# A sixth pair of row tiles in block products, and the last slots of a fused attention and mixer kernel rearranged

## The chip, the cores and the metric

The kernel runs on one core of one Trainium2 chip. The metric is the device time of one execution in microseconds (us). The kernel takes and gives float32; inside, the operands of its matmuls are float16 and the sums float32. The engines are called TensorE (PE in the profile), VectorE (DVE), ScalarE (ACT), GpSimd (POOL) and SyncE (SP, which only issues transfers here).

## The reference

Cosine attention over 8 batches, 12 heads, 448 rows and 64 columns, then a mixer of two parts: one over the rows (tokens), one over the columns (channels).

```python
q_n = q / (norm(q) + 1e-6); k_n = k / (norm(k) + 1e-6)
attn = softmax(q_n @ k_n.T / tau)
x = (attn @ v), heads side by side                  # [8, 448, 768]
h = max(x.T @ w_tok1, 0) @ w_tok2                   # 448 -> 256 -> 448
u = x + h.T
out = u + max(u @ w_ch1, 0) @ w_ch2                 # 768 -> 1536 -> 768
```

## The kernel before

**Slots.** Two heads of a batch make a pair; there are 48 pairs, six to a batch. The loop runs over them, and pass i is called slot i here. The order of all instructions is written out by hand: each engine works through its own queue in the order of the program. In slot i TensorE makes the scores of pair i (`score`, `score_rest`; exponentials on ScalarE), attention times v of pair i-1 (`pv_rest`, `pv`; VectorE divides with `rec` and writes `x`), the token mixer's second layer of pair i-2 (`tok2`, VectorE writes `u`) and its first layer of pair i-1 (`tok1`, VectorE writes `rt`). `side` holds what the other engines do for later pairs: GpSimd casts v, squares k and scales k and q (`kq`), VectorE sums the squares, SyncE loads and transposes.

**The channel mixer fills the slots.** `WORK` says which parts go into which slot. `ch1(b, ct)` is one of the 12 column blocks of the first layer of batch b (six matmuls of 448 columns, ReLU on ScalarE into `gt`). `ch2(b, m, n)` is one half (384 columns) of the second layer for row tile m of batch b: 12 matmuls, `psF`, and a VectorE add of u. A row tile has 128 rows. Two batches have 896 rows, so tiles of an odd batch are shifted by 64, and tile (b, 3) holds the last 64 rows of batch b-1 and the first 64 of batch b. Its add of u was made in two parts of 64 partitions, from the u of either batch.

**Block products.** For a pair of row tiles r1 and r2, `sg_first` and `sg_second` replace the four halves by seven products of six matmuls of 384 columns each (`sg_prod`), from sums of the tiles (`sg_sum` on GpSimd, tiles sg0 to sg2) and sums of the weights (`tw`). `FIRST` and `SECOND` say in which slots. In the slot of `sg_first` stand product 1 (`psY`) and 2 (`psX`) ahead of score_rest, 6 behind it, and 7 behind tok1; in that of `sg_second` products 5 (`psZ`) and 4 (`psW`) ahead of score_rest and 3 (again `psZ`) near the end. VectorE adds each to the output rows (`osg`).

**PSUM.** Pool `ps` (tag "b") has two buffers of a bank, `ps2` (tag "s") three of two banks. A tile of a pool waits until the buffer's last reader is done: psO of the two heads, psX, psW, psU (tok2), psR (tok1) and psT (transposes of u) take turns in "b"; scores, psY, psZ and the tail's `px`, `py`, `pz` in "s".

**The tail.** Batches 6 and 7 have their first layer in block products too, over both batches at once, behind slot 47: `prod1`, in steps `p1` to `p7`, each for d = 0, 1, 2. They read sums of the weights (`fast_weights1`: n = 1 writes s1w, 2 writes s2w from it, 3 rewrites a quarter of wc1t, 4 writes s4w), and differences of u (`fast_x`: t1x to t4x). Pair 47's u is transposed on TensorE (`upose`) for them. `fast_g` makes the sums for the second layer (`s1g`, `s2g` first). One helper records most elementwise operations of VectorE and GpSimd, so that they share line 544 in the profile before; the tiles tell them apart.

Of the kernel before, what the change touches and what calls it, by code (L numbers as in the profile page):

```python
# [22 lines left out]
def kernel(  # L23
# [12 lines left out]
    nc = tc.nc  # L36
# [455 lines left out]
    def m_ch2(b, m, lo, hi, st, wide):  # L492
# [10 lines left out]
        def add(p0, p1, bb, slot):  # L503
            nc.vector.tensor_tensor(out=o[p0:p1, lo:hi].rearrange("p (j e) -> p j e", e=128),
                                    in0=psF[p0:p1, 0:hi - lo].rearrange("p (j e) -> p j e", e=128),
                                    in1=u16[bb][p0:p1, lo // 128:hi // 128, slot], op=ALU.add)

        if m < 3:
            add(0, 128, b, m + b % 2)
        else:  # L510
            add(0, 64, b - 1, 3)
            add(64, 128, b, 0)
# [101 lines left out]
    def u_shared():  # L614
        nc.sync.dma_start(out=u16[B1][0:64, :, 0], in_=u16[B0][0:64, :, 3])
# [89 lines left out]
    def sg_first(r1, r2):  # L705
# [22 lines left out]
        return head, middle, end  # L728
# [187 lines left out]
    with tc.manual_schedule():  # L916
# [154 lines left out]
        for i in range(NPAIR + 1, NP_ALL):  # L1071
# [48 lines left out]
            if second:  # L1120
                second[1]()
# [155 lines left out]
```

## Time and profile before

| | us |
|---|---|
| median of 3 runs | 378.15 |
| lowest, highest | 377.91, 379.19 |
| the profiled execution | 377.93 |
| its span, first to last instruction | 376.1 |
| TensorE busy | 360.6 |
| GpSimd busy | 293.4 |
| VectorE busy | 260.5 |
| ScalarE busy | 251.5 |

The profiled execution is one run; the durations of single instructions come from it. In a row of the timeline stand start, duration, engine, line, operation and tiles, and in brackets how long the engine had been idle and what ended that. A busy time of TensorE includes some 0.2 us in which a matmul's result is still under way; the chain counts from one result to the next. The mean granted clock of TensorE was 0.997 of full.

### The profile page before, as it was taken

What the parts mean: (1) busy time and instruction counts of PE and PEld (TensorE: products, weight loads), DVE (VectorE), ACT (ScalarE), POOL (GpSimd) and SP (SyncE); (2) the same over time, 40 slices, a digit from 0 to 9 for tenths busy, and PEclk for the clock granted to TensorE, in tenths of its full rate; (3) what the DMA queues carried; (4) which work ended last, traced back from release to release, by engine and by line L of the source; (5) the groups of instructions that cost most, each with busy time, mean ns of one, the idle gap of its engine ahead of it and who ended that gap; (6) DMA issues with size and microseconds to landing.
All of it is one profiled execution on the core that took longest, in us unless ns stands there. A gap on an engine that the chain in (4) does not pass through costs nothing.

```text
span 376.1 us, 10388 instructions
## 1 busy us (share of the span) xinstructions
PE 360.6 (96%) x4060; PEld 236.0 (63%) x4060; DVE 260.5 (69%) x589; ACT 251.5 (67%) x440; POOL 293.4 (78%) x405
## 2 busy tenths in 40 slices
PE   6788999999999999999999999999999969999995
PEld 5566666676666766666666766666666646556663
DVE  7789765776556763875864876646777698786873
ACT  5999887857788597666677755978688434265110
POOL 8899998989989987878766887469989962345753
PEclk9999999999999999999999999999999999999998
DMA  7999999988989798879898979979875713103344
GB/s 200 270 254 197 265 255 205 208 149 163 231 206 198 163 246 173 178 171 237 163 204 187 162 182 214 225 172 182 196 148 124 150 40 99 22 3 91 89 125 126
DMA packets 118224, 64.64 MB, mean 172 GB/s; under 512 B 74272, under 2 KB 114848, under 8 KB 118176
## 3 DMA queue, kind: packets, MB, share of 16 engines
q1 hardware_dynamic: 111984, 58.25, 71.1%
q0 software_dynamic: 5616, 5.21, 8.8%
q8 instruction: 31, 0.51, 0.6%
q10 hardware_dynamic: 576, 0.52, 0.5%
q14 instruction: 17, 0.14, 0.1%
HBM read 43.45 MB, written 11.01 MB: 145 GB/s over the span
## 4 chain that ended last, share of the span: by engine, by line
PE 86%; DVE 5%; ACT 5%; DMA 1%; issue 1%; POOL 0%; SPq 0%; DVEq 0%; ACTq 0%
PE psG L483 22%; PE psO L402 9%; PE psF L500 8%; PE psS L363 8%; PE psU L452 5%; PE psR L438 5%; PE psYo L790 4%; PE psY L686 3%; ACT pt L364 3%; PE psY L598 3%; PE psXo L790 3%; PE psZo L790 3%; PE psZ L686 2%; PE psZ L598 2%; PE psX L598 2%; PE psQ L370 2%
## 5 line engine op out<-in xcount | busy, mean ns | idle before, releaser
L364 ACT ACTIVATE pt<-psS 128x896 f16<-128x896 f32 (+1 forms) x156 | 135.7, 911 | 28.3 <-PE psS L363 28.2
L483 PE MATMUL psG<-ut,wc1t 128*128 128x448 f16 x432 | 90.1, 352 | 0.0
L316 POOL TENSOR_TENSOR kq<-kf,rn 128x384 f16<-128x384 f32 (+1 forms) x43 | 38.0, 885 | 35.0 <-DVE rn L293 34.2
L483 PEld LDWEIGHTS <-wc1t 128*128 128x128 f16 x432 | 40.4, 97 | 32.0
L486 ACT ACTIVATE gt<-psG 128x448 f16<-128x448 f32 x72 | 38.9, 541 | 30.6 <-PE psG L483 30.6
L280 DVE TENSOR_REDUCE ssq<-sq 128x15 f32<-128x960 f32 (+2 forms) x45 | 49.9, 1111 | 2.9 <-ACT sq L262 2.9
L441 DVE TENSOR_SCALAR rt<-psR 128x256 f16<-128x256 f32 x48 | 20.1, 418 | 43.6 <-PE psR L438 43.6
L363 PE MATMUL psS<-qk 64*128 64x448 f16 x312 | 41.2, 354 | 4.4 <-DVE qk L342 3.0
L316 POOL TENSOR_TENSOR kq<-qf,rn 112x512 f16<-112x512 f32 x41 | 42.8, 1044 | 2.8
L455 DVE TENSOR_TENSOR u<-psU,x 128x512 f16<-128x512 f32 x48 | 33.1, 689 | 12.4 <-PE psU L452 11.4
L402 PE MATMUL psO<-vt,pt 128*128 128x65 f16 (+1 forms) x1024 | 39.2, 194 | 0.0
L406 DVE TENSOR_TENSOR x<-psO,rec 128x256 f16<-128x256 f32 x82 | 34.8, 424 | 2.8
L402 PEld LDWEIGHTS <-pt 128*128 128x128 f16 (+1 forms) x1024 | 34.2, 97 | 3.5 <-issue 0.9
L500 PE MATMUL psF<-wc2t,gt 128*128 128x384 f16 x192 | 33.8, 326 | 0.0
L264 POOL TENSOR_TENSOR sq<-kf 128x384 f32<-128x384 f32 (+1 forms) x35 | 30.0, 857 | 0.1
L452 PE MATMUL psU<-rt,w2t 128*128 128x128 f16 x384 | 29.4, 220 | 0.6 <-POOL w2t L211 0.6
L452 PEld LDWEIGHTS <-w2t 128*128 128x128 f16 x384 | 24.8, 98 | 8.0 <-DVE rn L293 0.8
L438 PEld LDWEIGHTS <-w1t 128*128 128x128 f16 x384 | 24.8, 98 | 7.9 <-issue 2.1
L438 PE MATMUL psR<-x,w1t 128*128 128x128 f16 x384 | 29.3, 219 | 0.2 <-DVE u L455 0.2
L371 ACT ACTIVATE pt<-psQ 128x448 f16<-128x448 f32 x36 | 19.6, 544 | 12.3 <-PE psQ L370 12.2
L324 POOL TENSOR_SCALAR kq<-kr,rn 64x64 f16<-64x64 f32 x72 | 22.7, 315 | 3.6
L363 PEld LDWEIGHTS <-qk 64*128 64x128 f16 x312 | 12.6, 94 | 19.0 <-issue 6.3
(164 smaller groups left out, 654.5 us busy)
## 6 DMA issues: line engine op xcount, KB each, us to landing
qf<-in_q_dram SPq DMA_DIRECT2D x43, 224.0 KB, 3.9
vf<-in_v_dram SPq DMA_DIRECT2D x36, 192.0 KB, 3.6
kf<-in_k_dram SPq DMA_DIRECT2D x34, 192.0 KB, 3.7
wc1t<-in_moe_w_ch_dram POOLq DMA_DIRECT2D x4, 576.0 KB, 10.5
wc2t<-in_moe_w_ch_dram POOLq DMA_DIRECT2D x2, 1152.0 KB, 12.7
kf<-in_k_dram SPq DMA_DIRECT2D x9, 224.0 KB, 8.4
vf<-in_v_dram SPq DMA_DIRECT2D x9, 224.0 KB, 8.3
kr<-in_k_dram SPq DMA_DIRECT2D x24, 48.0 KB, 3.6
```

Source lines behind the costliest of these rows:

```text
L280: nc.vector.tensor_reduce(out=st["ssq"][0:n, sl], in_=st["sq"][0:n, sl], axis=AXX.X, op=ALU.add)
L316: eng.tensor_tensor(out=kq[0:p, a, 0:n].rearrange("p c g e -> p g c e"), in0=st["kq"[a]][:].rearrange("p (g c) e -> p g c e", g=2), in1=_b ...
L363: nc.tensor.matmul(psS[:, hh, 0:S], qk[hb, c * n:c * n + 128], qm[hb], start=True, stop=True)
L364: nc.scalar.activation(out=pts[i % 2][0:n, 2 * S * c:2 * S * (c + 1)].rearrange("p (h s) -> p h s", h=2), in_=psS[0:n, :, 0:S], func=AF.Ex ...
L402: nc.tensor.matmul(psO[:, m, 0:E + 1], pts[i % 2][0:n, at:at + 128], vt[0:n, i % HP, nch * hh + c, 0:E + 1], start=(old(i) and c == 0), st ...
L406: nc.vector.tensor_tensor(out=st["x"][:, :, hh * E:(hh + 1) * E], in0=psO[:, :, 0:E], in1=_bcast_free(rec[:], E), op=ALU.mult)
L438: nc.tensor.matmul(psR[:, tt], w1t[:, w1[m], tt * 128:(tt + 1) * 128], st["x"][:, m], start=(m == 0), stop=(m == 3))
L452: nc.tensor.matmul(psU[:, m], w2t[:, tt, lo:lo + 128], st["rt"][:, tt], start=(tt == 0), stop=(tt == TT - 1))
L483: nc.tensor.matmul(psG[:, 0:S], wc1t[:, dt, ct * 128:(ct + 1) * 128], ut[b][:, dt].rearrange("p m s -> p (m s)")[:, lo:lo + S], start=(dt ...
L486: nc.scalar.activation(out=gt[:, ct, (b % 2) * S:(b % 2 + 1) * S], in_=psG[:, 0:S], func=AF.Relu)
L500: nc.tensor.matmul(psF[:, 0:hi - lo], gt[:, ct, at:at + 128], wc2t[:, ct, lo:hi], start=(ct == 0), stop=(ct == CT - 1))
L790: nc.tensor.matmul(out[:, o:o + hi - lo], a[:, j], fast_w2(n, j)[:, lo:hi], start=(start and j == 0), stop=(j == HC - 1), skip_group_check ...
```

## The change

- Tiles (2, 0) and (3, 3) become a sixth pair `G[5]`: their four halves in slots 26, 32 and 33 go, and products 1, 2, 6, 7, 5, 4 stand in slot 33, product 3 in slot 34. Tile (3, 2) has both its halves in slot 32.
- The pairs in `AHEAD` (`G[4]` and `G[5]`) have products 5 and 4 at the end of the first slot and no longer in the second. Product 5 goes into a "b" bank and is added to both output tiles; product 3 starts a bank of its own (`psV`).
- The first layers of batches 2 to 4 are spread anew over slots 21 to 38, the pairs G[1] and G[2] move to slots 29, 30 and 37, 38, and their GpSimd sums with them. In slot 32 ScalarE squares k.
- `u_shared` now copies the 64 shared rows of u into the odd batch in slots 16, 28 and 40, so that the add of a shared tile is one instruction.
- In slot 47, s1g and s2g (`fast_g`) are made behind product 3, where they stood in slot 46, and `p1(0)` stands ahead of tok1(46). s1w (GpSimd) moves from slot 46 to 47, s2w (VectorE) from slot 47 to behind pv of pair 47, and s4w from GpSimd in slot 47 to VectorE behind the t's of the second block of u.

```diff
-        def add(p0, p1, bb, slot):
...
-        if m < 3:
-            add(0, 128, b, m + b % 2)
-        else:
-            add(0, 64, b - 1, 3)
-            add(64, 128, b, 0)
+        nc.vector.tensor_tensor(out=o[:, lo:hi].rearrange("p (j e) -> p j e", e=128),
+                                in0=psF[:, 0:hi - lo].rearrange("p (j e) -> p j e", e=128),
+                                in1=u16[b][:, lo // 128:hi // 128, (m + b % 2) % 4], op=ALU.add)
...
-    def u_shared():
-        nc.sync.dma_start(out=u16[B1][0:64, :, 0], in_=u16[B0][0:64, :, 3])
+    def u_shared(b=B1):
+        nc.sync.dma_start(out=u16[b][0:64, :, 0], in_=u16[b - 1][0:64, :, 3])
...
-        at = [(slice(0, 128), b, m + b % 2)] if m < 3 else [(slice(0, 64), b - 1, 3), (slice(64, 128), b, 0)]
-        for p, bb, slot in at:
-            tt(nc.vector, j3(out[p]), j3(src[p, 0:DH]), u16[bb][p, HD * h:HD * (h + 1), slot], ALU.add)
+        tt(nc.vector, j3(out), j3(src[:, 0:DH]), u16[b][:, HD * h:HD * (h + 1), (m + b % 2) % 4], ALU.add)
...
-    def sg_second(r1, r2):
+    def sg_second(r1, r2, split=False):
         def head():
             st = slot_g[r1]
-            z = st["z"] = ps2.tile([128, 512], FP32, name=f"psZ_{r1[0]}_{r1[1]}", tag="s")
+            z = st["z"] = (ps if split else ps2).tile([128, 512], FP32, name=f"psZ_{r1[0]}_{r1[1]}",
+                                                      tag="b" if split else "s")
             o2 = st["o"][1]
             sg_prod(5, r1, r2, z)
             sg_add(o2[:, DH:D], z, o2[:, DH:D])
+            if split:
+                o1 = st["o"][0]
+                sg_add(o1[:, DH:D], z, o1[:, DH:D])
+                del st["z"]
...
-            sg_prod(3, r1, r2, st["z"], False)
-            sg_add(o1[:, DH:D], st["z"], o1[:, DH:D])
+            z = ps2.tile([128, 512], FP32, name=f"psV_{r1[0]}_{r1[1]}", tag="s") if split else st["z"]
+            sg_prod(3, r1, r2, z, split)
+            sg_add(o1[:, DH:D], z, o1[:, DH:D])
...
-    G = [((1, 1), (1, 2)), ((2, 1), (2, 2)), ((3, 0), (3, 1)), ((4, 0), (4, 1)), ((4, 2), (5, 3))]
+    G = [((1, 1), (1, 2)), ((2, 1), (2, 2)), ((3, 0), (3, 1)), ((4, 0), (4, 1)), ((4, 2), (5, 3)), ((2, 0), (3, 3))]
...
-        21: run(2, 0, 3), 22: run(2, 3, 7), 23: run(2, 7, 10), 24: run(2, 10, 11), 25: run(2, 11, 12),
-        26: halves(2, 0), 27: run(3, 0, 3), 28: run(3, 3, 4), 29: run(3, 4, 5),
-        30: run(3, 5, 9), 31: run(3, 9, 12), 32: [ch2(3, 3, 0), ch2(3, 2, 0)], 33: [ch2(3, 3, 1), ch2(3, 2, 1)],
-        34: run(4, 0, 1), 35: run(4, 1, 2), 36: run(4, 2, 5), 37: run(4, 5, 9), 38: run(4, 9, 12),
+        21: run(2, 0, 3), 22: run(2, 3, 6), 23: run(2, 6, 8), 24: run(2, 8, 9), 25: run(2, 9, 10),
+        26: run(2, 10, 12), 27: run(3, 0, 3), 28: run(3, 3, 6), 29: run(3, 6, 7),
+        30: run(3, 7, 8), 31: run(3, 8, 12), 32: halves(3, 2), 33: [],
+        34: run(4, 0, 2), 35: run(4, 2, 5), 36: run(4, 5, 8), 37: run(4, 8, 10), 38: run(4, 10, 12),
...
-    FIRST = {24: G[0], 28: G[1], 34: G[2], 41: G[3], 46: G[4]}
-    SECOND = {25: G[0], 29: G[1], 35: G[2], 45: G[3], 47: G[4]}
+    FIRST = {24: G[0], 29: G[1], 33: G[5], 37: G[2], 41: G[3], 46: G[4]}
+    SECOND = {25: G[0], 30: G[1], 34: G[5], 38: G[2], 45: G[3], 47: G[4]}
...
-    for g, at in zip(G, ((22, 23, 24, 25), (26, 27, 28, 29), (32, 33, 34, 35), (39, 40, 41, 42), (46, 46, 45, 47))):
+    for g, at in zip(G, ((22, 23, 24, 25), (27, 28, 29, 30), (35, 36, 37, 38), (39, 40, 41, 42), (46, 46, 45, 47), (32, 32, 33, 34))):
...
-    ACT_K = (14, 19, 20)
+    AHEAD = (G[4], G[5])
+    ACT_K = (14, 19, 20, 32)
...
-            if i == NP_ALL - 1:
-                fast_weights1(2, nc.vector)
             side(i)
+            if i in (16, 28, 40):
+                u_shared(i // NPAIR - 1)
             if i == NP_ALL - 2:
                 cast_v(i + 1)
+            if i == NP_ALL - 1:
                 fast_weights1(1, nc.gpsimd)
...
             if first:
                 tok1(i - 1)
                 first[2]()
+                if ahead:
+                    sg_second(*first[3], True)[0]()
...
             if second:
                 second[1]()
+            if i == NP_ALL - 1:
+                fast_g(0, 1)
+                fast_g(0, 2)
+                p1(0)
             if not first:
                 tok1(i - 1)
...
-            if i == NP_ALL - 2:
-                fast_g(0, 1)
-                fast_g(0, 2)
-            if i == NP_ALL - 1:
-                fast_weights1(4, nc.gpsimd)
         last = NP_ALL - 1
         fw["room"] = {}
-        p1(0)
         pv_rest(last)
...
+        fast_weights1(2, nc.vector)
         fast_weights1(3, nc.vector)
...
         for k in (2, 3, 4):
             fast_x(k, 1, 2)
+        fast_weights1(4, nc.vector)
         p1(2)
```

More of the change, by code (lines that the diff above doesn't have):

```diff
@@ L501, in m_ch2 @@
                              start=(ct == 0), stop=(ct == CT - 1))
-        def add(p0, p1, bb, slot):
-            nc.vector.tensor_tensor(out=o[p0:p1, lo:hi].rearrange("p (j e) -> p j e", e=128),
-                                    in0=psF[p0:p1, 0:hi - lo].rearrange("p (j e) -> p j e", e=128),
-                                    in1=u16[bb][p0:p1, lo // 128:hi // 128, slot], op=ALU.add)
-        if m < 3:
-            add(0, 128, b, m + b % 2)
-        else:
-            add(0, 64, b - 1, 3)
-            add(64, 128, b, 0)
+        nc.vector.tensor_tensor(out=o[:, lo:hi].rearrange("p (j e) -> p j e", e=128),
+                                in0=psF[:, 0:hi - lo].rearrange("p (j e) -> p j e", e=128),
+                                in1=u16[b][:, lo // 128:hi // 128, (m + b % 2) % 4], op=ALU.add)
         if st is None:
@@ L726, in end @@
                 sg_add_u(st["o"][1][:, DH * h:DH * (h + 1)], st["y"], r2, h)
-        return head, middle, end
-    def sg_second(r1, r2):
+        return head, middle, end, (r1, r2)
+    def sg_second(r1, r2, split=False):
         def head():
             st = slot_g[r1]
-            z = st["z"] = ps2.tile([128, 512], FP32, name=f"psZ_{r1[0]}_{r1[1]}", tag="s")
+            z = st["z"] = (ps if split else ps2).tile([128, 512], FP32, name=f"psZ_{r1[0]}_{r1[1]}",
+                                                      tag="b" if split else "s")
             o2 = st["o"][1]
@@ L1095 @@
             first = sg_first(*FIRST[i]) if i in FIRST else None
-            second = sg_second(*SECOND[i]) if i in SECOND else None
-            if first or second:
-                (first or second)[0]()
+            second = sg_second(*SECOND[i], SECOND[i] in AHEAD) if i in SECOND else None
+            ahead = first and first[3] in AHEAD
+            if first:
+                first[0]()
+            elif second and SECOND[i] not in AHEAD:
+                second[0]()
             elif todo:
```

## The prediction

> **What bounds the kernel now.** I read the page first, then busy time by stretch, TensorE's waits, the timeline from 296 us on, and the chain.
>
> ```profile
> PE 360.6 (96%) x4060; PEld 236.0 (63%) x4060; DVE 260.5 (69%) x589; ACT 251.5 (67%) x440; POOL 293.4 (78%) x405
> ```
>
> ```profile
> 60.00:296.00 236.00, 235.96 (x2777) 155.54 (x2774) 155.34 (x380) 174.19 (x319) 194.79 (x295) 1.00 0.90 186
> ...
> 300.00:304.00 4.00, 3.18 (x55) 2.12 (x52) 3.55 (x8) 2.18 (x3) 4.00 (x2) 1.00 0.54 133
> 304.00:309.00 5.00, 2.92 (x26) 1.68 (x23) 4.87 (x9) 0.90 (x2) 1.43 (x2) 1.00 0.00 2
> 309.00:320.00 11.00, 11.00 (x113) 7.07 (x113) 8.87 (x20) 4.59 (x5) 4.07 (x1) 1.00 0.34 86
> ```
>
> The second column is TensorE: from 60 to 296 us it is never idle, so a matmul taken out there is worth its full issue time. The only hole behind the start lies at 300 to 309 us (slots 46 and 47), where VectorE, the fourth column, is full: 4.87 of 5.00. TensorE's waits there:
>
> ```profile
> PE psW L686 <- DVE x L406: 1.6, 1, 1.6
> PE psS L363 <- ACT pt L364: 0.8, 1, 0.8
> PE psZ L686 <- DVE osg L544: 0.5, 1, 0.5
> ```
>
> The timeline says what VectorE does then, and how tight its queue is behind:
>
> ```profile
> 298.81 4.54 POOL L544 TENSOR_TENSOR s1w<-wc1t 128x2304 f16<-128x2304 f16 x1
> ...
> 301.52 2.26 DVE L544 TENSOR_TENSOR osg<-psY,u 64x384 f32<-64x384 f32 x4 [0.38 <-PE psY L686]
> ...
> 303.31 1.64 POOL L544 TENSOR_TENSOR sg<-gt,sg 128x768 f16<-128x768 f16 x1
> 303.81 1.56 DVE L544 TENSOR_TENSOR s1g<-gt 128x768 f16<-128x768 f16 x1
> ...
> 307.09 1.35 DVE L544 TENSOR_TENSOR s2w<-s1w,wc1t 128x2304 f16<-128x2304 f16 x1
> ...
> 312.42 0.18 DVE L405 RECIPROCAL rec<-psO 128x4 f32<-128x4 f32 x1 [1.40 <-PE psO L402]
> ...
> 318.90 0.69 DVE L455 TENSOR_TENSOR u<-psU,x 128x512 f16<-128x512 f32 x1
> ...
> 319.84 0.39 PE L468 MATMUL psT<-id,u 128*128 128x128 f16 x4
> ...
> 332.72 0.55 DVE L544 TENSOR_TENSOR room<-gt 128x768 f16<-128x768 f16 x1
> ```
>
> From 312.42 to 319.59 VectorE has no gap, and the last transpose (psT of pair 47) starts 0.25 us after its u is ready. I measure the end of the change's effect at that transpose: behind it TensorE runs without a wait to 371 us before, and the instructions are the same after.
>
> **Term 1, the sixth pair.** Tiles (2,0) and (3,3) cost four halves, in the chain 1.95 us each:
>
> ```profile
> 166.74 1.95 PE psF L500 x12
> ...
> 179.60 0.97 PE psY L686 x6
> ```
>
> that is 7.80 us; seven products of 0.975 make 6.83. In the full stretch that is -0.97 us.
>
> The pair's four GpSimd sums (1.64 each) go to slots 32, 32, 33 and 34. GpSimd's own slot is 4.22 us (0.83 + 0.72 + 1.05 + 0.50 + 0.83 + 0.29); slot 32 gives its K squares (1.12) to ScalarE and takes 3.28, so 6.4 us in a slot of 6.65. ScalarE has no ReLU there (3.9 us, and some 0.7 by its 0.63 for a 112x512 square). No cost. The moved first layers leave slots 23 and 26 with two column blocks, 5.1 us. The slot at 261.1 to 266.2 us, two blocks and a sum, is that case now:
>
> ```profile
> 261.10:266.20 5.10, 5.10 (x70) 3.45 (x67) 3.56 (x10) 4.86 (x10) 4.43 (x7) 1.00 0.80 191
> ```
>
> TensorE is full in it. GpSimd, 0.7 us over in slot 23, catches up in slot 24 (7.9 us), and what it makes is read two slots on. Zero; bounds 0 and +0.4 (the backlog, once uncovered).
>
> The three u_shared copies take SyncE's queue 0.64 us each (L615 in this trace) and land in 2.4; their readers are three slots or more behind, and only the u transpose of the same slot stands behind them. SyncE needs about 4.8 us of a slot of 5.1 or more. Zero; if that cover fails, up to 0.6 each. The adds of (1,3) and (3,3), no longer split into two of 0.55, take work off VectorE where nothing waits for it: zero as well.
>
> **Term 2, products ahead in slot 33.** Products 5 and 4 now stand at the end of the slot, in the two banks that the next slot's psO needs. In slot 24 product 7 was readable at 156.86 and VectorE added it at 156.90, two adds in 1.02 (0.46 from start to start). Behind them come two adds of product 5, then that of product 4: readable at +1.95 us, added until +2.60. TensorE has finished product 4 at +1.78 and the three scores (0.57) at +2.36, and meets the bank at +2.60: a wait of 0.24 us. Bounds 0 (scores slower) and 0.5 (one more add late). I take +0.24.
>
> **Term 3, slots 46 and 47.** In the times of before, as if slot 46 began when it did: product 7 issues until 301.32, product 5 until 302.29, product 4 until 303.27, scores until 303.84. The same wait holds psO to 304.08; pv ends at 305.04. x of the first head is ready at 305.50 and frees the bank of tok2(45): a wait of 0.33, tok2 until 306.00, product 3 until 306.98, p1(0) until 308.11, tok1(46) until 308.56. VectorE meanwhile adds u (306.2) and product 3 (307.2), then s1g and s2g at 0.55 each (307.7 to 308.85), no longer 1.56 (now it starts beside GpSimd's sum and ends 0.43 behind that sum's end; the room row of that shape, with GpSimd idle, has 0.55), since s1w ends on GpSimd before: the sum ahead of it waits for product 6 (299.6) and ends at 301.3, s1w 4.54 later at 305.8. Then rt(46) until 309.28. Because p1(0) now stands ahead of tok1, nothing covers rt: pv of pair 47 waits 0.77 for that bank and ends at 310.29, where before it ended at 312.60. So far 2.3 us are gained.
>
> Now VectorE's queue: reciprocal at 310.11, s2w at 311.22 (the same 1.11 behind as before), then the pitches of before: 1.27 to w(1,0)'s difference, 1.27 to t1x, 0.77 to u(46), 0.60 to rt, 0.33 to the three t, 0.90 to the copy, 0.45 to three more t, 0.91 to their end: 317.72. There s4w, on GpSimd before (4.55), takes 1.27 more, and u(47) runs from 318.99 to 319.68. TensorE has its work done at 314.59 and waits 0.68 for u(46), and at 318.19 and waits 1.5 for u(47). The copies that t2x needs of u(45) are issued at 306.9, eight us ahead of it. The transpose starts at 319.73 instead of 319.84: -0.11. The gain of the hole is spent by s2w and s4w in front of u. Bounds: -1.0 (pitches 0.1 shorter over nine instructions) and +0.6 (one more dependent add in that queue).
>
> **Sum.** -0.97 + 0.24 - 0.11 = -0.84 us on the profiled execution's 377.93 (span 376.1 and 1.8 around it): 377.09. The median of the runs shown is 0.22 above that execution, so 377.3.
>
> **Rivals.**
> *VectorE lets go sooner.* If TensorE's own work ended last ahead of the two transposes of u, its waits of 0.68 and 1.5 would go: the stretch ends at 317.55, 2.2 us earlier, which is 375.1 in all; half of it gives 376.2. For it: rows with neighbours were up to 0.05 shorter in pitch than alone. Against: 9 us of queue without a gap. Chance 0.24, faster.
> *GpSimd holds VectorE up (slower).* s1g stands 1.9 us behind the end of s1w. If s1w starts more than 1.9 us late, s1g waits out the rest, up to 4.5 us, and behind s1g on its engine stand s2g, rt(46) and with it pv of pair 47 and all that follows. At half, 2.3 us, it is 379.6; all of it gives 381.8. It decides from s1w ending past 309.7, where the loss passes 0.84 + 1.13 us. For it: s1g lost 1.0 us beside a GpSimd sum in this trace. Against: 1.9 us of cover. Chance 0.12. The Trainium skill ("SBUF — State Buffer", section "SBUF: two separate sides") has this as a rule: a VectorE instruction with two SBUF inputs and a GpSimd one that reads SBUF exclude each other, and the second waits until the first is done. The trace agrees with it, 1.56 against 0.55 us.
> *The six matmuls save nothing,* since slots 33 and 34 lose them again: VectorE has 8.0 us of work in the 8.6 of slot 33, and each further add late holds psO 0.5. Then 378.1 to 378.3. Chance 0.06, same.
>
> **Numbers.** The forecast has 0.58. Its own range, 376.7 to 378.0, crosses the line of faster: 0.3% of 378.15 is 1.13 us, about what a measurement of this kernel can tell from no change, so faster is below 377.02. I give 0.18 of it to faster, 0.40 to same. Faster 0.18 + 0.24 = 0.42; same 0.40 + 0.06 = 0.46; slower 0.12. The range of 8 in 10 runs from 375.8, which leaves out a third of the first rival, to 378.8, which leaves out the second.
>
> **What would show it.** TensorE's waits: psO on an add of osg once near 216 to 220 us (0.2), and in slots 46 and 47 on osg, x and rt; then psT on u twice, the second over 1 us. s1g at 0.55. psW's wait of 1.6 gone. VectorE without a gap from pv of pair 47 to the last u. I am wrong if psT waits for nothing, if TensorE has idle time of over 0.5 us anywhere from 60 to 290 us, or if s1w ends behind the start of s1g.

## The result, and the profile after

| | before | after |
|---|---|---|
| median of all runs, us | 378.85 (22 runs) | 380.93 (22 runs) |
| lowest run, us | 377.74 | 378.98 |
| first profiled execution, us | 377.93 | 381.87 |
| second profiled execution, us | 378.34 | 380.47 |

The ratio is 1.0045, 95% interval [1.0025, 1.0064]: slower by 1.7 us, where 0.8 us less was forecast. The slowest run after, 385.21 us, counts as a slow one and is not in the ratio. The time lies outside the range, on the other side of no change.

The page's busy times, and busy time by stretch (the second figure after the comma is TensorE's):

```profile
PE 361.8 (95%) x4054; PEld 236.4 (62%) x4054; DVE 260.9 (69%) x590; ACT 251.9 (66%) x442; POOL 294.3 (77%) x406
```

```profile
60.00:125.00 65.00, 64.39 (x773) 42.42 (x771) 41.23 (x101) 48.93 (x89) 57.45 (x87) 1.00 0.98 187
125.00:150.00 25.00, 25.00 (x298) 16.55 (x297) 15.69 (x39) 19.44 (x37) 22.43 (x32) 1.00 0.89 192
150.00:175.00 25.00, 23.23 (x283) 15.30 (x282) 17.33 (x42) 16.88 (x32) 18.56 (x31) 1.00 0.98 198
175.00:300.00 125.00, 124.89 (x1449) 81.84 (x1449) 83.02 (x203) 90.78 (x166) 103.86 (x153) 1.00 0.86 180
```

The six matmuls are gone (4054 in place of 4060). But the stretch in which TensorE was never idle before has two holes now, 0.6 us near 92 and 1.8 us at 150 to 175. TensorE's waits, there and in the last slots:

```profile
PE psS L363 <- DMA qk<-kq: 2.3, 2, 1.7
```

```profile
PE psT L468 <- DVE u L455: 1.9, 2, 1.4
PE psO L385 <- DVE rt L441: 0.4, 1, 0.4
PE psU L452 <- DVE x L406: 0.2, 1, 0.2
```

The hole at 150 us is slot 24's first score: it waits for the transposed queries and keys (`qk`) that SyncE fetches. The timeline ahead of it, SyncE's queue (SPq), GpSimd's last scaling of that pair and TensorE's score:

```profile
141.00 1.41 SPq L348 DMA_TRANSPOSE qk<-kq  x1
142.50 0.53 SPq L153 DMA_DIRECT2D qf<-in_q_dram  x1
143.09 0.46 SPq L135 DMA_DIRECT2D kf<-in_k_dram  x1
143.60 1.41 SPq L143 DMA_DIRECT2D kr<-in_k_dram  x2
...
143.99 1.04 POOL L316 TENSOR_TENSOR kq<-qf,rn 112x512 f16<-112x512 f32 x1
...
145.05 0.60 SPq L135 DMA_DIRECT2D vf<-in_v_dram  x1
145.69 1.27 SPq L143 DMA_DIRECT2D vr<-in_v_dram  x2
147.06 2.06 SPq L461 DMA_TRANSPOSE ut<-u  x1
149.24 1.23 SPq L348 DMA_TRANSPOSE qk<-kq  x1
...
152.35 0.74 PE L363 MATMUL psS<-qk 64*128 64x448 f16 x6 [1.71 <-DMA qk<-kq]
```

GpSimd is done with pair 24's `kq` at 145.03. Its transpose stands in the queue behind that of pair 23, five loads (seven issues) and a transpose of u, and is issued 4.2 us later; 3.1 us after that it has landed, and TensorE starts 0.05 us behind. SyncE had no pause in these eight us. The same rows before, where TensorE waits for nothing: `kq` is ready at 142.37, its transpose issued 1.9 us later, and slot 24 begins 7.8 us behind `kq`:

```profile
141.33 1.04 POOL L316 TENSOR_TENSOR kq<-qf,rn 112x512 f16<-112x512 f32 x1
...
142.88 1.23 SPq L461 DMA_TRANSPOSE ut<-u  x1
144.23 1.25 SPq L348 DMA_TRANSPOSE qk<-kq  x1
...
150.17 0.74 PE L363 MATMUL psS<-qk 64*128 64x448 f16 x6
```

**Slot by slot.** A slot is measured from its first `psS` to the next slot's. Lengths agree within 0.02 us between executions where nothing waits, so what a slot is longer than its shortest is a wait. The second pair of profiled executions is the clean one: slot 14 begins at 83.54 before and at 83.55 after (in the first pair they are 1.96 us apart from the start on, by instructions that the change doesn't touch: in the first profile after, the granted clock was 0.50 from about 23 to 26 us).

| us | before | after | difference | of it work moved or saved | waits |
|---|---|---|---|---|---|
| slots 17 to 21 | 31.99 | 32.46 | +0.47 | 0 | 0.47 |
| slots 22 to 26 | 35.10 | 32.74 | -2.36 | -3.81 | 1.45 |
| slot 27 | 6.23 | 7.42 | +1.19 | 0 | 1.19 |
| slots 28 to 45 | 116.63 | 119.56 | +2.93 | +3.81 - 0.88 | 0 |
| slot 46 to the end | 81.64 | 81.80 | +0.16 | +0.16 | |

So the sixth pair saved about what it should, 0.88 us, the end gave nothing, and 3.1 us went into waits in slots 17 to 27. (Of the +0.16 at the end, -0.17 stands ahead of the last transpose of u and +0.33 in the closing instructions behind the landing of the last store.) 3.81 us of TensorE's work left slots 22, 23 and 26 (1.13, 1.13 and 1.55) for slots 28 and later.

### The profile page after: what moved, and what is told of

Read it like the earlier page. It is cut to its first block, busy times and chain, and to the rows that moved or that the text cites. A ratio compares the mean times of both kernels' runs of the same rounds, so it can differ in the third digit from the quotient of the medians.

```text
span 380.1 us, 10384 instructions
## 1 busy us (share of the span) xinstructions
PE 361.8 (95%) x4054; PEld 236.4 (62%) x4054; DVE 260.9 (69%) x590; ACT 251.9 (66%) x442; POOL 294.3 (77%) x406
## 4 chain that ended last, share of the span: by engine, by line
PE 78%; DMA 8%; DVE 6%; POOL 2%; ACT 2%; issue 1%; SPq 0%; DVEq 0%; POOLq 0%
PE psG L483 20%; PE psO L402 8%; PE psS L363 7%; PE psF L500 5%; PE psU L452 5%; PE psR L438 5%; PE psY L679 4%; PE psYo L787 4%; DMA kf<-in_k_dram 4%; PE psY L591 3%; PE psZ L679 3%; PE psXo L787 3%; PE psZo L787 3%; DMA qk<-kq 2%; DVE ssq L280 2%; PE psQ L370 2%
## 5 line engine op out<-in xcount | busy, mean ns | idle before, releaser
L483 PEld LDWEIGHTS <-wc1t 128*128 128x128 f16 x432 | 40.2, 97 | 31.6
L264 POOL TENSOR_TENSOR sq<-kf 128x384 f32<-128x384 f32 (+1 forms) x34 | 29.2, 857 | 0.9 <-DMA kf<-in_k_dram 0.8
L500 PE MATMUL psF<-wc2t,gt 128*128 128x384 f16 x144 | 25.4, 326 | 0.0
```

The source lines that it names most:

```text
L483: nc.tensor.matmul(psG[:, 0:S], wc1t[:, dt, ct * 128:(ct + 1) * 128], ut[b][:, dt].rearrange("p m s -> p (m s)")[:, lo:lo + S], start=(dt ...
L500: nc.tensor.matmul(psF[:, 0:hi - lo], gt[:, ct, at:at + 128], wc2t[:, ct, lo:hi], start=(ct == 0), stop=(ct == CT - 1))
```

## The experiments

In the table, waits are the profiled execution's time over the shortest length of the same slots with the same work.

| kernel | ratio to before, 95% | slots 14, 17 | 21 to 26 | 27 | elsewhere |
|---|---|---|---|---|---|
| changed kernel (first, second profile) | 1.0045 [1.0025, 1.0064] | 0.7, 0.1 | 1.8, 1.7 | 0.2, 1.2 | |
| e1 middle undone | 0.9988 [0.9958, 1.0018] | 0.3 | 0 | 0 | |
| e2 end undone | 1.0025 [0.9993, 1.0057] | 1.0 | 1.5 | 0.55 | |
| e12 before, work shifted alone | 1.0037 [1.0002, 1.0072] | 0.7 | 1.0 | 0 | |
| e3 slot 23 refilled | 1.0040 [1.0005, 1.0075] | 2.5 | 4.7 | 0 | |
| e4 stores of slot 20 late | 1.0080 [1.0047, 1.0114] | 0.6 | 1.55 | 1.5 | |
| e5 loads a slot later | 1.0019 [0.9992, 1.0046] | 0.3 | 0 | 1.3 | 0.3 in 44 |
| e7 slots 22 to 25 as before | 1.0049 [1.0017, 1.0082] | 0.5 | 0.2 | 2.5, with 26 | |
| e9 loads behind u | 1.0009 [0.9977, 1.0041] | 0 | 4.2 | 0 | 0.45 in 32 |
| e10 both | 1.0041 [0.9999, 1.0083] | 0.4 | 0 | 0.7 | 0.8 in 36, 44 |
| e11 before, order of e9 | 0.9984 [0.9954, 1.0015] | 0.1 | 0 | 0 | |
| e13 slot 22 full, 24 empty | 1.0054 [1.0019, 1.0088] | 0.6 | 1.2 | 1.3 | |
| e14 and u of slot 25 first | 1.0006 [0.9983, 1.0029] | 2.5 | 0.7 | 0.1 | |
| e8 shared tiles in two parts | 1.0087 [1.0055, 1.0120] | 0.1 | 0.15 | 1.5 | 1.3 in 34, 0.9 from 46 on |

### Where the cost sits: e1, e2, e12

```diff
-    FIRST = {24: G[0], 29: G[1], 33: G[5], 37: G[2], 41: G[3], 46: G[4]}
+    FIRST = {24: G[0], 28: G[1], 34: G[2], 41: G[3], 46: G[4]}
...
-    AHEAD = (G[4], G[5])
-    ACT_K = (14, 19, 20, 32)
+    AHEAD = (G[4],)
+    ACT_K = (14, 19, 20)
```

> The changed kernel with the whole middle as it was before: five pairs, the sixth pair's halves in slots 26 and 32, and the old shares of layer 1 in slots 22 to 38. Kept of the change: the copies of u in slots 16, 28 and 40, the single add per half, and the rearranged slots 46, 47 and after. Theory A (the lightened slots 22, 23 and 26 outrun SyncE's queue, so that slot 24 waits for its transposed queries and keys): slot 23 is 6.2 us again, slot 24 starts without a wait over 0.3 us, and the time is that of before within 0.4 us, rather below it (the end alone was 0.16 us shorter in the changed kernel's trace). Theory B (the cost arises before slot 16, for instance 2.7 us of shift that the profiled run has by slot 15): the cost stays, 1 to 2 us over before. Theory C (the copies of u or the rearranged end cost it): 1 to 2 us over before, with the wait in the profile after slot 40.

Ratio 0.9988, and no wait in slots 21 to 28. The copies of u and the new end, with the old middle, cost nothing that can be measured; the cost needs the new middle.

```diff
-    AHEAD = (G[4], G[5])
+    AHEAD = (G[5],)
...
+            if i == NP_ALL - 2:
+                fast_g(0, 1)
+                fast_g(0, 2)
+            if i == NP_ALL - 1:
+                fast_weights1(4, nc.gpsimd)
```

> The changed kernel with its end as before: only the sixth pair runs its product 5 ahead, the last pair doesn't, and the sums of the first-layer weights, the two sums over x and the first product of the last batch stand where they stood before. The middle and the copies of u are kept. Theory A: TensorE still waits 1 to 2.5 us for the transposed queries and keys at slot 24, and the time is that of the changed kernel plus 0 to 0.3 us, so still about 2 us over before. Theory C (the end costs it): the time falls by 1.5 us or more, to that of before. Theory B: as the changed kernel.

The waits at slots 24 and 27 stayed (1.50 and 0.55 us) and the ratio is 1.0025. This fits the first theory; against the changed kernel the intervals overlap, so the ratios say nothing of the end's own worth. The profiles do: from the start of slot 46 to the last transpose of u it is 24.95 us here, with the old end, and 25.18 and 25.20 with the new one (25.33 and 25.37 in the kernel before). By these profiles the rearranged end is 0.2 us longer than the old one would be in the changed kernel.

e12 starts from the kernel before:

```diff
-        21: run(2, 0, 3), 22: run(2, 3, 7), 23: run(2, 7, 10), 24: run(2, 10, 11), 25: run(2, 11, 12),
-        26: halves(2, 0), 27: run(3, 0, 3), 28: run(3, 3, 4), 29: run(3, 4, 5),
-        30: run(3, 5, 9), 31: run(3, 9, 12), 32: [ch2(3, 3, 0), ch2(3, 2, 0)], 33: [ch2(3, 3, 1), ch2(3, 2, 1)],
+        21: run(2, 0, 3), 22: run(2, 3, 6), 23: run(2, 6, 8), 24: run(2, 8, 9), 25: run(2, 9, 10),
+        26: run(2, 10, 12), 27: run(3, 0, 3), 28: run(3, 3, 4), 29: run(3, 4, 5),
+        30: run(3, 5, 9) + [ch2(2, 0, 0)], 31: run(3, 9, 12) + [ch2(2, 0, 1)], 32: [ch2(3, 3, 0), ch2(3, 2, 0)], 33: [ch2(3, 3, 1), ch2(3, 2, 1)],
```

> The kernel before with nothing of the change but the lightening of the slots: the shares of layer 1 of slots 22 to 26 as the change has them, and the two halves of the tile (2,0) moved from slot 26 to slots 30 and 31. No sixth pair: every matmul of before is there, 3.8 us of them later. If nothing but TensorE's work counted, the time would be that of before within 0.3 us. Theory A: waits of 1.2 to 3 us for transposes at slots 23 to 28, none of them in the kernel before, and the time 1 to 3 us over before: the price of the change without its gain. If it is that of before, theory A falls and the cost lies in the sixth pair's own products and sums.

One sum of pair G[1] is made in slot 26 here ahead of the last two blocks of layer 1, from values that are not final; the instruction is the same. Ratio 1.0037: with every matmul of before still there, the shift alone costs about as much as the whole change (1.4 and 1.7 us). Its timeline shows the new wait at the same place:

```profile
149.51 0.74 PE L363 MATMUL psS<-qk 64*128 64x448 f16 x6 [0.94 <-DMA qk<-kq]
```

So shortening slots 22, 23 and 26 costs by itself, without a sixth pair. That it is the whole cost is not shown. Of the 1.7 us of waits in this profile 0.7 stand in slot 14, ahead of the edit, and slot 27 has none; and the changed kernel, which saves 0.88 us, must lose about 2.6 to end 1.7 over before, against the 1.4 here (by the interval 0.1 to 2.7).

### How far waits vary: both kernels again

> The kernel before, unchanged, for a second profile of it. Theory L: no wait over 0.3 us at slots 21 to 27; a wait of up to 1 us may show at slots 14 and 17, where the first trace has 0.1 to 0.8 us to spare for the transposes of pairs 18 and 19. If waits of 1 us or more stand at slots 23 to 27 here too, the waits there are not the change's.

> The changed kernel, unchanged, for a second profile of it. Theory L: 1.1 to 2.3 us of waits for transposes at slots 23 to 27 in sum, as slots 22 and 23 leave 5.5 us after the keys and queries of pair 24 are ready, and the queue and flight of before took 6.7; the place may be the start of slot 24, of slot 25 or the first block in slot 27. None over 0.3 us at slots 28 to 45.

The kernel before is as expected. The changed one waits 2.65 us at slots 23 to 27, where 1.1 to 2.3 was expected, and 0.28 in slot 21. Slots 23 and 27, before and then after, in busy time by stretch:

```profile
144.02:150.25 6.23, 6.23 (x75) 3.99 (x73) 3.56 (x9) 5.40 (x11) 4.43 (x7) 1.00 0.98 163
...
171.75:177.98 6.23, 6.23 (x75) 4.06 (x74) 3.66 (x10) 5.21 (x10) 5.45 (x9) 1.00 1.04 252
```

```profile
143.36:149.92 6.56, 5.17 (x70) 3.41 (x69) 4.91 (x11) 5.07 (x10) 5.89 (x11) 1.00 0.63 123
...
169.86:177.28 7.42, 6.29 (x75) 4.01 (x74) 3.56 (x9) 5.53 (x11) 7.25 (x12) 1.00 1.20 218
```

The kernel before has TensorE busy for all of both; the changed one is idle for 1.39 of 6.56 and 1.13 of 7.42 us. From these four executions comes the account of a single transpose:

| us | before | before again | after | after again |
|---|---|---|---|---|
| pair 24: `kq` ready to slot 24, TensorE not waiting | 7.80 | 7.78 | 5.53 | 5.53 |
| in SyncE's queue | 1.86 | 2.01 | 4.21 | 3.85 |
| in flight | 4.8 | 4.4 | 3.1 | 3.1 |
| to spare | 1.1 | 1.4 | -1.8 | -1.4 |
| u of pair 23: ready to the sixth `psG` of slot 27, not waiting | 11.1 | 11.1 | 9.5 | 9.5 |
| in SyncE's queue | 4.77 | 4.80 | 4.78 | 4.79 |
| in flight | 4.7 | 4.6 | 5.0 | 6.0 |
| to spare | 1.6 | 1.7 | -0.3 | -1.3 |

`kq` of pair 24 is ready 5.8 us after slot 22 begins in all four, whatever the slot's length: a shorter slot does not bring it earlier, it only calls for the result earlier. What is to spare in the kernel before (1.1 to 1.4 us) is less than the 2.26 us that slots 22 and 23 lose; the 1.6 for u is just what slot 26 loses (1.55), and flights vary by more than that is left. The queue is another matter. Pair 23's transpose, one slot earlier, already queued 2.2 and 1.9 us in the changed kernel's two profiles, against 0.8 and 0.9 before. And e12, with the same light slots, has pair 24 in the queue for 2.1 us, about as before. So the shift alone cost slot 24 about 1 us; the 1.4 to 1.8 of the changed kernel come with a queue that was longer ahead of these slots.

### Giving the latency back: e3, e7, e13, e14

```diff
-        21: run(2, 0, 3), 22: run(2, 3, 6), 23: run(2, 6, 8), 24: run(2, 8, 9), 25: run(2, 9, 10),
+        21: run(2, 0, 3), 22: run(2, 3, 6), 23: run(2, 6, 9), 24: [], 25: run(2, 9, 10),
```

> The changed kernel with one block of layer 1 (six matmuls, about 1.1 us) moved from slot 24 to slot 23, so that slot 23 has three blocks as before the change and slot 24 none. The work is the same in sum. Theory A: slot 23 covers 1.1 us more of SyncE's delay, the wait at slot 24 falls from 1.8 us to about 0.7 us, slot 24 is 1.1 us shorter (unless the next transpose is late in its turn, at slot 25, which would show as a new wait there), and the time falls by 0 to 1.1 us, likeliest 0.7. Theories B and C: no change within 0.3 us.

The wait at slot 24 went, a new one of 0.69 stood in slot 25 (a score's bank on an add of `osg`), and this execution lost 4.0 us in slot 21, ahead of the edit. No gain; inconclusive by itself, all the more as the profiled execution is the longest of its twelve.

e7:

```diff
+        21: run(2, 0, 3), 22: run(2, 3, 7), 23: run(2, 7, 10), 24: run(2, 10, 11), 25: run(2, 11, 12),
+        26: [], 27: run(3, 0, 3), 28: run(3, 3, 6), 29: run(3, 6, 7),
```

> The changed kernel with four, three, one and one blocks of layer 1 in slots 22 to 25 as in the kernel before (the change had three, two, one, one and two in slot 26); slot 26 is left with none. The matmuls are the same in sum; only 2.3 us of them go back from after slot 24 to before it. Theory A: slots 22 and 23 are 7.37 and 6.24 us again, no wait at slot 24; slot 26 is 5.10 us, and a wait of 0 to 1.5 us may stand at slot 27 on the transposes of u. The time falls by 0.5 to 2 us against the changed kernel, to that of before or down to 0.9 us below it. Theory B and C: no change within 0.3 us.

The wait at slot 24 is gone (0.05), but the wait on u in slot 27 was larger than I expected, 2.5 us with slot 26. I had that slot's length wrong: with no block it is 2.83, not 5.10 us, so u had 3.8 us less than before.

e13:

```diff
+        21: run(2, 0, 3), 22: run(2, 3, 7), 23: run(2, 7, 9), 24: [], 25: run(2, 9, 10),
```

> The changed kernel with four, two, none, one and two blocks of layer 1 in slots 22 to 26 (the change: three, two, one, one, two). The sum is the same; slots 22 and 23 together are 12.47 us in place of 11.34. Theory L, which the traces so far lead to: what binds is a latency. The queries and keys of pair 24 are ready 5.8 us after slot 22 begins in every trace; then comes the wait in SyncE's queue (1.9 us in the kernel before, 4.2 in the changed one) and the flight of the transpose (3.1 to 4.8 us). Slots 22 and 23 leave 7.8 us for that in the kernel before and 5.5 in the changed one, here 6.7. With the queue and flight of before (6.7 us) the wait at slot 24 is 0 to 0.3 us, with those of the changed kernel's trace (7.3) 0.6. The wait at slot 27 stays (0.2 to 1.3 us). Time 0.5 to 1.8 us below the changed kernel, ratio to before 0.998 to 1.003. The rival, that it is throughput of the DMA engines or SyncE from slot 14 to 28, expects no gain over 0.4 us.

At slot 24 it did what the account says: 6.67 us allowed, 2.72 queued and 3.8 in flight, no wait. But 0.69 in slot 25, 0.49 ahead of slot 27 and 1.27 in it took its place. Ratio 1.0054: no gain.

e14 is e13 and this; `loads` holds the slot's `load_qk` and `load_v`, and in slot 25 it and product 4's store stand behind tok2:

```diff
+            if i not in range(25, 26):
+                loads(i)
...
                 tok2(i - 2)
+            while stores:
+                stores.pop(0)()
+            if i in range(25, 26):
+                loads(i)
```

> The run before this one, and in slot 25 alone the transpose of u of pair 23 ahead of that slot's loads and of product 4's store. Theory L: the transpose of u of pair 23 is issued within 2.5 us of u (4.8 us in the kernel before and in the changed one), lands 2 us earlier, and slot 27 has no wait (6.23 us); slot 24 as in the run before. Time 0.3 to 1 us below the run before, which would make it 0.2 to 0.9 us faster than the kernel before. The throughput rival: waits come back at slots 28 to 31, no gain.

The transpose of u of pair 23 is issued 2.7 us behind u in place of 4.8, and slot 27 is 6.37 us, forecast 6.23. No wait came back at slots 28 to 31, where the throughput rival wanted one. The ratio is 1.0006: the changed kernel's loss is about gone, but it is no faster than before. Its profile has 2.5 us of waits in slots 14 and 17 and 0.7 in 25.

### Relieving SyncE: e4, e5, e9, e10, e11

e4 (`put` collects the stores of `ost` in `held` while the mark is set):

```diff
+            if i in (20,):
+                pipe["hold"] = True
...
+            pipe.pop("hold", None)
+            if i == 24:
+                while held:
+                    held.pop(0)()
```

> The changed kernel with the six stores that slot 20's two halves issue held back and issued in slot 24 (queue of SyncE, and one of ScalarE's with them). They took some 7 us of SyncE's time between 136 and 141 us in the profiled run, ahead of the transpose that slot 24 waited for. Nothing else moves. Theory A: the transposed queries and keys of pair 24 land 3 us or more earlier, TensorE does not wait at slot 24, slot 23 is 5.1 to 5.3 us, and the time falls by 1.5 to 3 us, to 378 or 379 where before has 378.9; new waits may arise at slots 25 to 27, where the stores now lie ahead of other transposes, and give back up to 1 us. Theories B and C: no change within 0.3 us.

Slot 23 is 5.10 us and slot 24 starts without a wait, as expected; but slot 26 is 1.55 longer (the transpose of pair 27's queries and keys stands behind the held stores) and slot 27 1.54 (u of pair 23 was written at 161.34 and its transpose issued at 170.23, behind the held stores among others). That is 3.1 us where I allowed 1, and the time rose.

e5:

```diff
-            if i + 6 < NP_ALL and i + 2 >= DMA_T0:
-                load_qk(i + 6)
+            ahead_qk = 6 if i < 20 else 5
+            if i != 20 and i + ahead_qk < NP_ALL and i + 2 >= DMA_T0:
+                load_qk(i + ahead_qk)
```

> The changed kernel, in which slot 20 loads no queries and keys and every later slot loads those of five pairs ahead in place of six. From slot 20 on one pair's loads (416 KB and, in some slots, the rest rows) are out of SyncE's queue and off the DMA engines that were ahead of the transposes; the squares that need them come two slots later. So far each profile of a kernel with the new middle showed waits of TensorE for transposes between slots 14 and 28 (1.2 to 3.8 us in sum beside the few in the kernel before), so theory A is now: from slot 14 to 28 SyncE's queue issues without a gap and the 16 DMA engines are over 0.9 busy, so that taking TensorE's work out of slots 22, 23 and 26 buys waits. Theory A: no wait at slots 21 to 27, slot 23 5.1 us, slot 27 6.23 us, time 1 to 2.5 us below the changed kernel, that is 378 to 379.5 where before has about 379; if a wait stays, at slots 14 to 17, ahead of the edit. Theory B (start) and C (end and copies): no change within 0.3 us.

Half as expected: no wait at slots 21 to 26 (pair 24 spends 0.08 us in the queue), 1.3 us at slot 27. Its timeline shows why; u of pair 23 was written at 161.58:

```profile
162.40 1.23 SPq L348 DMA_TRANSPOSE qk<-kq  x1
163.72 0.54 SPq L153 DMA_DIRECT2D qf<-in_q_dram  x1
164.32 0.44 SPq L135 DMA_DIRECT2D kf<-in_k_dram  x1
164.81 1.26 SPq L143 DMA_DIRECT2D kr<-in_k_dram  x2
166.12 0.60 SPq L135 DMA_DIRECT2D vf<-in_v_dram  x1
166.82 2.04 SPq L693 DMA_DIRECT2D out_dram<-osg  x2
168.96 1.26 SPq L461 DMA_TRANSPOSE ut<-u  x1
...
172.51 0.35 PE L483 MATMUL psG<-ut,wc1t 128*128 128x448 f16 x1 [1.24 <-DMA ut<-u]
```

Seven us in the queue, behind another pair's transpose and behind loads and a store that nobody was waiting for yet, then 3.5 in flight.

e9 is the order of e14 over slots 20 to 27, on the changed kernel's own shares; e10 is e9 and e5; e11 is e9's order in the kernel before:

```diff
+            if i not in range(20, 28):
+                loads(i)
```

> The changed kernel with another order in SyncE's queue alone: in slots 20 to 27 the loads of queries, keys and values, and the stores that a pair's product 4 lets go, are issued behind that slot's transpose of u instead of ahead of it. The same DMAs, the same bytes. Theory A1 (SyncE's in-order queue makes transposes late: in the run with loads a slot later the transpose of u of pair 23 was issued 7 us after u was written, behind five loads and a store of 2.0 us): the transpose of u of pair 23 is issued within 3 us of u, slot 27 is 6.2 to 6.4 us, the wait at slot 24 stays under 0.5 us as that slot's transpose has two loads fewer ahead of it, and the time falls by 1 to 2.5 us against the changed kernel, to about that of before. Theory A2 (the DMA engines, over 0.9 busy, bound the stretch whatever the order): the waits move but their sum stays within 0.7 us, and the time with it. Late loads could show as new waits of GpSimd on kf or vf.

> Both edits on the changed kernel: the order of the run before this one, and no loads of queries and keys in slot 20, those of five pairs ahead after it. Theory A1: no wait in slots 20 to 27 (slots 22, 23, 26, 27 of 6.23, 5.10, 5.10, 6.23 us); only what arises at slots 14 to 17 stays. The time is 0.9 us below that of before at best (377.5 to 378.5 where before has 378.9), ratio 0.996 to 0.999. Theory A2: 0 to 1 us below the run with later loads alone, the wait at slot 27 still over 0.7 us.

> The kernel before with the same order in SyncE's queue (loads and product 4's stores behind the transpose of u in slots 20 to 27). Its profile shows no wait of TensorE there, so the order has nothing to give back. Theory A1: within 0.3 us of before; over 0.5 us faster would mean that the kernel before, too, loses time there in executions that were not profiled, and the gain of the order in the changed kernel would then say less of the change.

e9 cured slot 27 (6.23 us) and moved the wait to slot 24: the loads of one slot now stand right ahead of the next slot's transpose of `kq`, which queued 4.8 us. The ratio, 1.0009, is nevertheless below the changed kernel's. e10 had no wait in slots 21 to 26, but 0.7 us in slot 27, which was to have none, and about 0.4 each in slots 17, 36 and 44. e11 did not change the kernel before. So no version of the sixth pair that I ran is faster than before.

### The copies of u: e8

```diff
-            if i in (16, 28, 40):
+            if i in (40,):
...
+            add(0, 64, b - 1, 3)
+            add(64, 128, b, 0)
```

> The changed kernel without the copies of u in slots 16 and 28 (96 KB, 0.66 us of SyncE's time each); tiles shared by two batches are added in two parts on VectorE as before. The one in slot 40 stays. Theory C, in the form that the copy in slot 16 is what delays the transposes: the slots after 16 show no wait (slot 17 was 0.3 to 1.25 us too long in four of five profiles that have the copy) and the time falls by 1 us or more, while the wait at slot 24 goes from 1.8 us to under 1 us. Theory A: the copy is one of some ten issues per slot, its removal takes 0.7 us off the wait at slot 24 and at slot 17 at most, and the two adds of 64 rows cost TensorE nothing or up to 0.5 us in slots 33 and 34; time 0 to 0.8 us below the changed kernel.

The wait at slot 24 fell to 0.15 (1.95 us in the queue), more than theory A allowed. But slot 27 waits 1.55, and slot 34 is 1.29 longer, by psO's bank on adds of `osg` (0.69 and 0.28); the last pair's add of the shared tile (5, 3) costs the same two waits in slot 47, and the stretch from slot 46 on is 0.9 longer. Ratio 1.0087: the copies pay for themselves.

That the copy in slot 16 makes the queue longer is likely, not shown. Without it, pair 24's transpose queued 1.9 to 2.4 us (before twice, e8, e11, e12); with it 1.7 in e1, 2.1 to 3.5 in e7, e13 and e14, and 3.9 to 4.2 in e2 and the changed kernel (e3, which lost 4.0 us in slot 21, had 0.03). Slot 18, two slots behind the copy, begins with a wait of 0.2 to 1.2 us for its queries and keys in nine of the fifteen profiles that have it, and in none of the five without.

### The same bytes by another queue: e6, e17, e18

e6 moves the rest rows, e17 the stores of slots 20 and 25 (issued in slots 24 and 29), e18 is e17 with slot 25's loads behind its transpose of u:

```diff
-            nc.sync.dma_start(out=t[64 * g:64 * g + 64],
+            (nc.scalar if i >= 2 * HP else nc.sync).dma_start(out=t[64 * g:64 * g + 64],
...
+            held.append(lambda: nc.scalar.dma_start(**what))
...
+            if i in (24, 29):
+                while held:
+                    held.pop(0)()
```

> The changed kernel with the loads of the rest rows (four issues in every third slot, about 2.7 us of SyncE's time) issued by ScalarE's queue from pair 6 on. The bytes and the DMA engines' work are the same; only SyncE is relieved. This parts theory A in two. A1, SyncE's issue order bounds the stretch: the transpose for slot 24 is issued 2.5 us earlier, the waits at slots 21 to 27 go, and the time falls by 1 to 2.5 us. A2, the DMA engines bound it: transposes are issued earlier but land as late, the waits stay within 0.5 us of the changed kernel's, and the time with them. By both ScalarE pays some 2.5 us in every third slot, of which none should reach TensorE while ScalarE is 66% busy; if it does, the profile shows it as waits of TensorE on ScalarE's exponentials.

> The changed kernel, in which the stores of slots 20 and 25 (eight issues, some 6.5 us of SyncE's time in the changed kernel's trace) are issued by ScalarE's queue in slots 24 and 29, where ScalarE has about 3 us idle behind its squares. The bytes are the same, the data long written. Theory A1 (SyncE's issuing: in the kernel before it issues 36.7 us and pauses 4.5 us in the 41.3 us of slots 22 to 27, in the changed kernel 34.3 us and 0.4 us in 37.5 of its own longer 39.4): SyncE pauses again, the transposes of queries and keys for pair 24 and of u for pair 23 are issued within 2 us of their data, no wait at slots 24 and 27 over 0.3 us, and the time falls by 1.5 to 2.5 us against the changed kernel, ratio to before 0.996 to 1.000. Theory A2 (the DMA engines): the waits stay within 0.7 us in sum, ratio 1.002 to 1.005. If ScalarE's issues delay its exponentials, TensorE's waits on ScalarE show it at slots 24 and 29.

> The run before this one, with slot 25's loads behind that slot's transpose of u (pair 23). Theory A1: as that run or up to 0.5 us below it, slot 27 of 6.23 us; ratio to before 0.995 to 1.000. Theory A2: as that run within 0.3 us, both over 1.002.

All three are slower: 1.079 [1.075, 1.083], 1.023 [1.018, 1.028] and 1.027 [1.023, 1.031]. ScalarE was held by its own issues (in e6, four loads at 102.7 us took 5.6 us of it). From e17's timeline (ACTq is ScalarE's queue):

```profile
154.06 3.65 ACTq L494 DMA_DIRECT2D out_dram<-ost  x3
...
187.55 7.47 ACTq L494 DMA_DIRECT2D out_dram<-osg  x4
...
195.66 0.38 PE L385 MATMUL psO<-vt,pt 64*128 64x65 f16 x7 [4.82 <-ACT gt L486]
```

Four stores whose data had long been written took 7.47 us to issue, and TensorE waited 4.8 us for ScalarE's next ReLU. In e17 slot 24 has no wait (0.91 us in the queue) and SyncE pauses again, but the stores also moved in time, as in e4; slot 25 is 1.65 us longer by ScalarE's stall, and u of pair 23 still queued 4.65 us where under 2 was expected. What is won in the queue is also lost in part behind it: pair 24's transpose was 4.4 to 4.9 us in flight in e4, e5, e10 and e17, which issued it within 1 us of its data, and 3.1 in the changed kernel, which issued it 4 us late (e6, with the rest rows in another queue, had 0.03 and 3.1). Whether the queue is slow because SyncE issues slowly, or because the DMA engines behind it make each issue wait, is therefore not settled. The Trainium skill ("Trainium Kernel Development and Optimization", section "Key Constraints") says that transfers of all queues share the same 16 DMA engines, so that a second issuing engine saves issue time alone; here SyncE's queue did become shorter, but ScalarE's own issues cost more than that.

## Why the prediction was wrong

**Term 1, the matmuls: right.** -0.97 forecast; slots 28 to 45 show -0.88, Term 2's wait in it.

**Term 1, the light slots: the step that failed.** "Zero; bounds 0 and +0.4" measured 2.0 and 2.9 us in slots 21 to 27 of the changed kernel's two profiles. Two sentences carried it. "TensorE is full in it" took slot 40 for the case of slot 23, but slot 40 stands where SyncE's queue is empty (it is 5.10 us in every profile but e6's). In the trace of before the transpose that slot 41 needs also had 5.5 us, but it queued 0.03 and was 3.1 in flight, so 2.4 were to spare. "SyncE needs about 4.8 us of a slot of 5.1" left out the stores and what an issue takes above its shortest. In the kernel before, SyncE pauses (gaps of over 0.2 us between its rows) for 4.5 and 3.7 us of the 41.3 us of slots 22 to 27 in its two profiles, so it needs over 6 us of a slot; in the changed kernel it pauses for 1.8 and 2.2 us of 39.5 and 40.2. The 3.8 us taken out of these slots came back as fewer pauses and as waits of TensorE. And a sum against a slot's length was the wrong test: each transpose has its own time from ready to needed, and the trace of before had all of it (7.8 us allowed, 1.9 queued, 4.8 in flight, 1.1 to spare, against 2.26 taken away).

**The copies: not settled.** Zero was forecast, up to 0.6 each "if that cover fails". In slot 17, behind the first copy, the changed kernel's two profiles have waits of 0 and 0.1, e2, the same up to slot 46, has 1.0; what the copy adds to pair 24's queue is only likely (see e8). "Only the u transpose of the same slot stands behind them" misread the queue: it is in order, so the next slots' transposes stand behind them too. "Take work off VectorE where nothing waits for it" was wrong to their credit: without them slot 34 loses 1.29.

**Term 2:** a wait of 0.24 forecast on the add of product 4. In the chain, psO's first part took 0.25 in slot 34 and 0.14 in slot 33, so 0.11 us, about half:

```profile
214.53 0.14 PE psO L385 x8
...
221.48 0.97 PE psW L679 x6
222.46 0.67 PE psS L363 x6
223.13 0.25 PE psO L385 x8
```

**Term 3: right.** From slot 46's start to the last transpose of u it is 25.33 us before and 25.18 after: -0.15, forecast -0.11. But e2, which has the old end and differs from the kernel before there only by the single add of the shared tile (5, 3), takes 24.95; so that add gained, and the rearrangement gave 0.2 of it back. The waits on x and on rt were 0.2 and 0.4 us, forecast 0.33 and 0.77. The timeline:

```profile
305.12 4.57 POOL L537 TENSOR_TENSOR s1w<-wc1t 128x2304 f16<-128x2304 f16 x1
...
311.45 0.55 DVE L537 TENSOR_TENSOR s1g<-gt 128x768 f16<-128x768 f16 x1
...
318.98 0.40 PE L468 MATMUL psT<-id,u 128*128 128x128 f16 x4 [0.51 <-DVE u L455]
...
321.44 1.35 DVE L537 TENSOR_TENSOR s4w<-wc1t,s2w 128x2304 f16<-128x2304 f16 x1
322.70 0.68 DVE L455 TENSOR_TENSOR u<-psU,x 128x512 f16<-128x512 f32 x1
323.45 0.40 PE L468 MATMUL psT<-id,u 128*128 128x128 f16 x4 [1.35 <-DVE u L455]
```

s1g took the 0.55 us of the `room` row, 1.8 us behind s1w's end (1.9 forecast), so GpSimd held nothing up and that rival falls. TensorE waits 0.51 and 1.35 for the two u (0.68 and 1.5 forecast): VectorE's queue sets the end, and the fast rival falls too. The third rival falls by the 0.88 us that slots 28 to 45 gained. No rival named the cause; it set off one of the prediction's own signs of being wrong, idle time of TensorE over 0.5 us between 60 and 290 us.

## What to carry to other kernels

Work that fills a slot is also cover for transfers: before moving it, take for each transfer needed in the next slots the time from its data being ready to its use, and subtract its queue and flight as the trace shows them; that TensorE waits for nothing doesn't say how little was to spare. An in-order queue is not judged by its mean load: look at whether it pauses, and what stands ahead of the urgent entry. When a saving of 0.9 us comes with a move of 3.8 us, the move has to be priced first.

## What the runs showed of the hardware

A wait can cost TensorE more than itself. In e9's slot 24 the score waited 2.54 us, and then the granted clock (the figure behind GpSimd's count) was 0.50 for some 3.4 us, so that slot 24 was 1.55 us too long as well. Busy time by stretch:

```profile
148.60:151.10 2.50, 0.04 (x1) 0.00 (x0) 1.48 (x2) 0.17 (x1) 2.50 (x6) 1.00 0.90 172
...
152.10:153.10 1.00, 1.00 (x22) 1.00 (x21) 0.18 (x1) 1.00 (x2) 0.56 (x1) 0.50 0.80 267
153.10:154.10 1.00, 1.00 (x12) 0.66 (x10) 0.91 (x4) 0.97 (x4) 0.00 (x0) 0.50 0.85 175
154.10:155.10 1.00, 1.00 (x5) 0.48 (x4) 0.46 (x3) 0.45 (x1) 0.42 (x1) 0.50 1.09 277
```

The same followed 2.24 us of idle in e3's slot 21, and 4.82 in e17's slot 30, where it lasted 6.8 us; after 1.39 and 1.71 us in the changed kernel's slot 24 the clock stayed at 1.00. The Trainium skill ("TensorE: Matmul & The Clock Gate", section "What's actually happening") has the clock halved after an idle window of about 3.4 us and full again after about 3.4 us of work. The half and the 3.4 us of e9 agree with it; the idle time does not. The Trainium skill's advice to avoid gaps over about 3 us (same page, section "Why this matters for your kernels") is too generous here, where 2.24 was enough.

The spread of the changed kernel's runs, 379 to 385 us, goes with the clock: nine of the 22 had a mean granted clock of 0.994 or less and took 381.8 to 385.2 us, the others 379.0 to 382.4. In the experiments' runs of the kernel before, 20 of 128 had 0.995 or less. So part of the 1.7 us may come by the clock. Whether waits in slots 14 to 27 lowered it there is not shown; in the one such run that has a profile, the first, it was down at about 23 to 26 us, ahead of the change.
